# Attention and soft MoE on one core: half tiles after 12 products, three stores on GpSimd's queue, 48 TensorE instructions fewer

## The chip, the cores and the metric

The kernel runs on one core of a Trainium2 chip. The core has a matrix engine (TensorE, PE in the profile; its weight loads are PEld), a vector engine (VectorE, DVE), a scalar engine (ScalarE, ACT), GpSimd (POOL), and SyncE (SP), which here only issues DMAs. The engines run side by side and wait for each other by semaphores; 16 DMA engines move data between the chip's memory and the core. The metric is the device time of one launch in microseconds (us); the time given for a kernel is the median of its runs.

## The reference

Softcapped attention over 8 batches and 12 heads, then a soft mixture of experts over its result, cut to what is computed:

```python
scores = scale * np.matmul(q, k.transpose(0, 1, 3, 2))      # q, k, v: 8 x 12 x 448 x 64
scores = cap * np.tanh(scores / cap)
attn = np.exp(scores - max); attn = attn / (sum + 1e-09)
x = np.matmul(attn, v) ... reshape(3584, 768)
logits = x @ phi                                            # 32 slots: 8 experts, 4 slots each
slot_input = softmax_over_tokens(logits).T @ x
for e in range(8):                                          # w1: 768 x 1024, w2: 1024 x 768
    slot_out[e] = np.maximum(slot_input[e] @ w1[e], 0.0) @ w2[e]
out = softmax_over_slots(logits) @ slot_out                 # 3584 x 768, float32
```

## The kernel before

The order of the instructions on each engine is written out by hand: engines take them in the order in which the Python text emits them.

The attention part runs over 56 chunks of six score tiles. `run(j, slot)` emits what `at(j, slot, ...)` has put into a table for chunk `j` and a place in it. Some of that is unused work for PE: `spare(n, parts)` takes a PSUM tile of `parts` x 128 columns and lets `busy` (L880) write products of ones there that nobody reads. With `parts` of 1 each product has 128 columns; with 3, `n // 3` products have 384 and the rest 128. Each product is two PE instructions, a weight load and a matmul.

Behind the attention comes the mixture of experts, from L1054 on. The second weights are held in blocks of four: `w2_parts` lists half 0 (columns 0 to 383) and then half 1 (384 to 767) of 16 groups. The first 11 groups of half 0 lie in `w2b`; the other 5 and all 16 of half 1 are brought back from memory into `w2t` by 21 loads on SP's queue (L1059). `layer1` multiplies the slots with the first weights, `h_transp` turns the result, and `layer2(n0, half)` adds four products to the 128 x 384 accumulator `so_ps[half]`; a half takes 16 calls, 64 products. ACT copies the finished half 0 to `so[0]` (L1168), DVE half 1 to `so[1]` (L1177).

An output tile is 128 tokens by 768 columns, and there are 28. For the first `NH` = 12 of them the halves are made apart. The loop at L1170 runs half 1 of `layer2`, and six times, between its calls, it makes two half tiles of half 0, one finished by ACT and the next by DVE: a product with `so[0]` (L1148), a multiplication by the tokens' weights into a tile `obh` (L1150, L1152), a store of 192 KB on SP's queue (L1136). Before the change the first such pair stands behind 16 products of half 1 and the others 8 products apart. Behind the copy to `so[1]` the loop at L1182 makes half 1 of the same 12 tiles, stored two at a time, and then the 16 whole tiles (`ob`, L1193 to L1206). Each engine issues its own DMAs in order; SP has all stores.

Of the kernel before, what the change touches and what calls it, by code (L numbers as in the profile page):

```python
# [37 lines left out]
def kernel(  # L38
# [31 lines left out]
    pe, dve, act, pool, sp = nc.tensor, nc.vector, nc.scalar, nc.gpsimd, nc.sync  # L70
# [673 lines left out]
    def et_tile(bb, c):  # L744
        return (ETl if bb == B // 2 - 1 else ET4[:, bb])[:, c, :, :].rearrange("p a q -> p (a q)")
# [50 lines left out]
    def at(j, slot, f, *a):  # L796
        if j < 0:
            j, slot = 0, "b"
        aux.setdefault((j, slot), []).append((f, a))
# [24 lines left out]
    for b in range(B):  # L824
        j, p = b * PER, 6 * b
# [31 lines left out]
    for n, job in enumerate(wjobs):  # L857
        at(1 + n * (NCH - 5) // len(wjobs), "b", *job)
    for j, slot, n in ((0, "a", 5), (0, "c", 16), (1, "b", 12), (1, "c", 3)):
        at(j, slot, spare, n, 1)  # L860
    LATE = ((52, 'd', 3, 1), (54, 'd', 3, 3),)
    for j, slot, n, parts in LATE:
        at(j, slot, spare, n, parts)
    at(34, "<b", fill, 7)
# [86 lines left out]
    def bank(shape, dt=F32, name="bank"):  # L951
        n = turns.pop(0)
        if not turns:
            turns.extend((3, 2, 6, 0, 1))
        return big.tile(shape, dt, name=name, tag=f"b{n}")
# [149 lines left out]
    def layer2(n0, half):  # L1105
        for n in range(n0, n0 + 4):
            i, ft, gg = blocks[n]
            pe.matmul(so_ps[half][32 * gg:32 * gg + NS, :],  # L1108
                      hpad[:, 4 * i + gg, ft, :],
                      w2_half(n, half),  # L1110
                      start=(n0 == 0), stop=(n0 == len(blocks) - 4))
# [18 lines left out]
    so_ps += [bank([P, HD], name=f"so_ps{half}") for half in range(2)]  # L1130
    obs, waiting = {}, {}

    def store(n, h0, h1, src, tokens=1):
        bb, c = divmod(n, NT)
        width = (h1 - h0) * HD
        sp.dma_start(out=bass.AP(tensor=out.tensor,  # L1136
                                 offset=(2 * bb * S + c) * D + h0 * HD,
                                 ap=[[NT * D, P], [1, tokens * D]] if width == D else
                                 [[NT * D, P], [D, tokens], [1, width]]),
                     in_=src)  # L1140

    def half_tile(n, half, home, eng):

        bb, c = divmod(n, NT)
        if c == 0:
            obs[bb, half] = wts.tile([P, NT, HD], F32, name="obh", tag="w1", bufs=E)
        ob = obs[bb, half][:, c, :]
        pe.matmul(home, et_tile(bb, c), so[half], start=True, stop=True)  # L1148
        if eng == "dve":
            dve.tensor_scalar_mul(ob, home, winv[:, bb, c:c + 1])  # L1150
        else:
            act.mul(ob, home, winv[:, bb, c:c + 1])  # L1152
        k = waiting.pop(half, n)
        if half and n + 1 < NH and c < NT - 1 and k == n:
            waiting[half] = n
            return
        store(k, half, half + 1, obs[bb, half][:, c - (n - k):c + 1, :], n - k + 1)

    NH = 12
    n2 = len(blocks)  # L1160
# [8 lines left out]
    done = 0  # L1169
    for n0 in range(0, n2, 4):  # L1170
        layer2(n0, 1)

        if n0 % 8 == 4 and n0 > 4 and done < NH:
            for eng in ("act", "dve"):
                half_tile(done, 0, bank([P, HD], name="op0"), eng)
                done += 1
# [5 lines left out]
    for n in range(B // 2 * NT):  # L1182
        bb, c = divmod(n, NT)
        if n == NH + 3:
            e_transp(B - 1)
        if n == NH + 5:
            e_transp(B - 2)
        op = fin.tile([P, 2, 512], F32, name="op", tag="op")
        if n < NH:
            half_tile(n, 1, op[:, 0, 0:HD], "act" if n % 2 else "dve")  # L1190
            continue
        for half in range(2):
            pe.matmul(op[:, half, 0:HD], et_tile(bb, c), so[half],  # L1193
                      start=True, stop=True)

        if n == NH or c == 0 or full:
            ob, n1 = wts.tile([P, 2, 2, HD], F32, name="ob", tag="w1", bufs=E), n
        dst = ob[:, n - n1, :, :]
        if n % 2:
            dve.tensor_scalar_mul(dst, op[:, :, 0:HD], winv[:, bb, c:c + 1])  # L1200
        else:
            act.mul(dst, op[:, :, 0:HD], winv[:, bb, c:c + 1])  # L1202
        full = n > n1 or c == NT - 1
        if full:
            store(n1, 0, 2, ob[:, 0:n - n1 + 1, :, :].rearrange("p t a d -> p (t a d)"),
                  n - n1 + 1)  # L1206
# [35 lines left out]
```

## Time and profile before

| | us |
|---|---|
| median of 3 runs | 283.15 (282.86 to 283.71) |
| the profiled execution | 283.45 |
| span of its instructions | 281.7 |
| ACT busy | 249.1 (88%) |
| PE busy | 246.5 (88%) |
| DVE busy | 239.5 (85%) |
| POOL busy | 140.9 (50%) |
| attention part, up to about | 237 |
| mixture of experts up to the first half tile | 237 to 251 |
| output tiles and their stores | 251 to 280 |

The profile shows one execution. Each engine's rows give start, length, line and operation; "idle" is the time for which an engine had nothing to do just before, with the instruction that released it; "issue" stands where the profile shows no such instruction. In the windows the DMA share is the busy time of the 16 DMA engines over the stretch; packets overlap a little, so it can exceed 1. The queue called q1 is SP's and ACT's, q0 is GpSimd's, and q8 carries instructions.

### The profile page before, as it was taken

Reading aid. Unit: us, or ns where it says so; the run is one execution under the profiler, and the core shown is the slowest. Engines: PE = TensorE matmul, PEld = TensorE weight load, DVE = VectorE, ACT = ScalarE, POOL = GpSimd, SP = SyncE. Lnnn points to the kernel's source line nnn. Section 1 sums busy time; section 2 is a strip of 40 time slices with the busy share of each in tenths; the row PEclk is TensorE's granted clock in tenths of the full one; section 3 lists DMA queues with packets and bytes.
Section 4 is the critical chain, followed back from the end, with each engine's and each line's share of the span. In section 5 each row is a group of like instructions: output and inputs, shape, how many; then the busy total and the mean of one; then the engine's idle time right before and its main releaser. Section 6 shows DMA issues by size and latency. Waiting matters only on the chain.

```text
span 281.7 us, 10449 instructions
## 1 busy us (share of the span) xinstructions
PE 246.5 (88%) x4563; PEld 167.0 (59%) x4563; DVE 239.5 (85%) x474; ACT 249.1 (88%) x198; POOL 140.9 (50%) x198
## 2 busy tenths in 40 slices
PE   8897889998998999889998999899988999997720
PEld 7555556756665766566656675667565777642410
DVE  3479999999999999999999999999999996447840
ACT  3999999999999999999999999999999997236730
POOL 7885548662957285727673768285744120200000
PEclk9999999999999999999999999999999999999995
DMA  7999999999999999999999999999999589959997
GB/s 245 245 190 203 218 211 227 228 223 217 206 218 225 219 231 226 225 216 213 221 226 215 207 220 230 217 219 214 231 217 220 128 260 317 408 201 391 413 424 303
DMA packets 58332, 68.08 MB, mean 242 GB/s; under 512 B 4144, under 2 KB 54448, under 8 KB 58288
## 3 DMA queue, kind: packets, MB, share of 16 engines
q0 software_dynamic: 42448, 35.31, 79.7%
q1 hardware_dynamic: 15552, 31.89, 32.4%
q8 instruction: 35, 0.57, 0.7%
q10 hardware_dynamic: 288, 0.23, 0.3%
q14 instruction: 9, 0.07, 0.1%
HBM read 91.72 MB, written 19.27 MB: 394 GB/s over the span
## 4 chain that ended last, share of the span: by engine, by line
ACT 38%; PE 31%; DVE 20%; issue 5%; POOL 1%; DVEq 0%; ACTq 0%
ACT ex L374 16%; ACT ex L366 14%; PE pv L635 8%; ACT ex L362 7%; PE sc L349 4%; DVE xq L645 2%; DVE xp L615 2%; PE so_ps L1108 2%; PE hp L1080 2%; DVE xp L613 2%; DVE ex L616 2%; ACT ob L1202 2%; PE op L1193 1%; DVE xf L612 1%; PE op L1148 1%
## 5 line engine op out<-in xcount | busy, mean ns | idle before, releaser
L366 ACT ACTIVATE ex<-sc 128x1344 f16<-128x1344 f32 (+1 forms) x91 | 118.5, 1405 | 1.5 <-PE sc L349 1.5
L374 ACT ACTIVATE ex<-ex 128x1344 bf16<-128x1344 f16 (+5 forms) x58 | 110.2, 1911 | 0.1
L635 PE MATMUL pv<-vbd,ex 128*128 128x130 bf16 (+1 forms) x1610 | 95.0, 212 | 9.5 <-POOL vbd L289 3.9
L635 PEld LDWEIGHTS <-ex 128*128 128x128 bf16 (+1 forms) x1680 | 75.6, 101 | 38.1 <-issue 6.2
L289 POOL CAST vbd<-vraw 64x896 bf16<-64x896 f32 x46 | 47.3, 1027 | 60.2 <-PE pv L635 42.5
L349 PE MATMUL sc<-qT,kT 64*64 64x448 bf16 x672 | 66.4, 359 | 5.6 <-ACT ex L366 4.1
L349 PEld LDWEIGHTS <-kT 64*64 64x64 bf16 x672 | 22.4, 105 | 14.4 <-ACT ex L366 6.3
L645 DVE TENSOR_TENSOR xq<-pv,rec 128x448 bf16<-128x448 f32 x46 | 28.7, 625 | 1.6
L362 ACT ACTIVATE ex<-sc 128x2688 f16<-128x2688 f32 x11 | 28.1, 2552 | 0.1
L615 DVE TENSOR_TENSOR xp<-xp,xf 128x1344 f16<-128x1344 f16 (+2 forms) x34 | 27.5, 808 | 0.5
L616 DVE TENSOR_TENSOR ex<-ex,xp 128x1344 uint16<-128x1344 uint16 (+2 forms) x34 | 26.9, 791 | 0.2
L613 DVE TENSOR_TENSOR xp<-xf 128x1344 f16<-128x1344 uint16 (+2 forms) x34 | 26.9, 790 | 0.2
L116 POOL DMA_DIRECT2D w1b<-in_moe_w_dram x32 | 25.8, 808 | 0.0
L281 DVE COPY kT<-kps 128x896 bf16<-128x896 bf16 x23 | 14.2, 616 | 4.9 <-PE kps L276 2.8
L610 DVE TENSOR_SCALAR ex<-ex 128x1344 uint16<-128x1344 f16 (+2 forms) x34 | 17.0, 501 | 1.2 <-ACT ex L362 0.7
L614 DVE TENSOR_SCALAR xp<-xp 128x1344 f16<-128x1344 f16 (+2 forms) x34 | 17.0, 500 | 0.6
L612 DVE TENSOR_SCALAR xf<-ex 128x1344 uint16<-128x1344 uint16 (+2 forms) x34 | 17.2, 507 | 0.3
L185 POOL DMA_DIRECT2D qb<-in_q_dram x22 | 16.3, 739 | 1.5 <-PE qps L279 0.9
L297 POOL MEMSET vbd<- 64x1 bf16 x22 | 3.0, 138 | 27.7 <-PE pv L635 27.4
L617 DVE TENSOR_SCALAR ex<-ex 128x1344 uint16<-128x1344 uint16 (+2 forms) x34 | 16.5, 484 | 0.2
L185 POOL DMA_DIRECT2D kb<-in_k_dram x22 | 16.5, 748 | 0.0
L120 POOL DMA_DIRECT2D w2d<-in_moe_w_dram x21 | 16.1, 789 | 0.0
(124 smaller groups left out, 320.6 us busy)
## 6 DMA issues: line engine op xcount, KB each, us to landing
w1b<-in_moe_w_dram POOLq DMA_DIRECT2D x32, 384.0 KB, 9.6
vraw<-in_v_dram SPq DMA_DIRECT2D x44, 224.0 KB, 6.3
w2d<-in_moe_w_dram POOLq DMA_DIRECT2D x21, 384.0 KB, 9.7
w2t<-w2d SPq DMA_DIRECT2D x21, 384.0 KB, 6.5
out_dram<-ob SPq DMA_DIRECT2D x7, 768.0 KB, 6.8
qb<-in_q_dram POOLq DMA_DIRECT2D x22, 224.0 KB, 8.1
kb<-in_k_dram POOLq DMA_DIRECT2D x22, 224.0 KB, 7.7
w2b<-in_moe_w_dram POOLq DMA_DIRECT2D x11, 384.0 KB, 8.9
```

Of the source, the lines that this page charges most:

```text
L116: pool.dma_start(out=w1b[e][:, js, fs], in_=w1r[:, e, js, fs])
L185: pool.dma_start(out=t, in_=quad_ap(nm, Q))
L289: pool.tensor_copy(vbds[Q % 2][r, :, :, c0:c0 + DH], raw[r])
L349: ins = pe.matmul(sc[cs, u, 0:S], qkT["k", Q][r, c, cs], qkT["q", Q][r, :, cs], start=True, stop=True).ins
L362: apart["t", i - 1] = apart["t", i] = act.activation(exs[j].bitcast(F16), own["board"][:, :, 0:S], ACT.Tanh, scale=qk_scale / cap).ins
L366: ins = act.activation(exs[j][:, half * CS + u0:half * CS + u1, :].bitcast(F16), (own[0] if i == u0 == 0 else sc)[:, u0:u1, 0:S], ACT.Tanh ...
L374: act.activation(exs[j][:, u0:u1, :], exs[j][:, u0:u1, :].bitcast(F16), ACT.Exp, scale=cap)
L613: lambda: dve.tensor_tensor(p, s, s.bitcast(F16), op=ALU.mult),
L615: lambda: dve.tensor_tensor(p, p, s, op=ALU.mult),
L616: lambda: dve.tensor_tensor(y, y, p, op=ALU.add),
L635: pe.matmul(out_, exs[j][r, u, q0:q0 + (HP if tail else P)], v_, start=(c == 0 and g == gs[0] < NF), stop=(c == NT - 1), skip_group_check= ...
L645: dve.tensor_tensor(xq[Q][:, h, s0:s1, :], pv[:, 0:s1 - s0, 0:DH], rec.to_broadcast([P, s1 - s0, DH]), op=ALU.mult)
```

## The change

```diff
     for j, slot, n in ((0, "a", 5), (0, "c", 16), (1, "b", 12), (1, "c", 3)):
-        at(j, slot, spare, n, 1)
-    LATE = ((52, 'd', 3, 1), (54, 'd', 3, 3),)
+        at(j, slot, spare, n)
+    LATE = ((52, 'd', 3, 3), (54, 'd', 3, 3),)
...
-    def store(n, h0, h1, src, tokens=1):
+    def store(n, h0, h1, src, tokens=1, queue=None):
...
-        sp.dma_start(out=bass.AP(tensor=out.tensor,
+        (queue or sp).dma_start(out=bass.AP(tensor=out.tensor,
...
-        store(k, half, half + 1, obs[bb, half][:, c - (n - k):c + 1, :], n - k + 1)
+        store(k, half, half + 1, obs[bb, half][:, c - (n - k):c + 1, :], n - k + 1,
+              pool if n in (1, 3, 5) and not half else None)
...
-        if n0 % 8 == 4 and n0 > 4 and done < NH:
+        if n0 % 8 == 0 and n0 > 0 and done < NH:
```

Three things change. The unused products of chunks 0 and 1, and three of chunk 52, are emitted with 384 columns where three can be joined: 39 products become 15, which is 48 PE instructions fewer, all of them ahead of the mixture of experts. The six pairs of half tiles stand behind 12, 20, 28, 36, 44 and 52 products of half 1 instead of 16, 24, 32, 40, 48 and 56, so that the last pair has 12 products behind it instead of 8. And the half-0 stores of tiles 1, 3 and 5, the ones that DVE finishes in the first three pairs, are issued by GpSimd instead of SP.

## The prediction

> **What bounds the kernel now.** I read the page first, then the last 40 us in windows, the chain of waits and the timeline around the code that changes, and last the DMA queues in short windows. The page:
>
> ```profile
> span 281.7 us, 10449 instructions
> PE 246.5 (88%) x4563; PEld 167.0 (59%) x4563; DVE 239.5 (85%) x474; ACT 249.1 (88%) x198; POOL 140.9 (50%) x198
> ...
> DMA  7999999999999999999999999999999589959997
> ...
> q8 instruction: 35, 0.57, 0.7%
> ```
>
> ACT and DVE fill the attention part; the last slices belong to the DMA engines. The windows of that end (span, then busy time of PE, weight loads, DVE, ACT, POOL; granted clock, DMA share, GB/s) and the stores' rows:
>
> ```profile
> 246.00:249.50 3.50, 3.50 (x93) 2.15 (x81) 2.00 (x9) 0.47 (x1) 0.00 (x0) 1.00 0.91 358
> 249.50:252.50 3.00, 2.53 (x36) 0.80 (x35) 0.86 (x2) 1.47 (x3) 0.00 (x0) 1.00 0.11 38
> 253.00:254.00 1.00, 1.00 (x15) 0.35 (x18) 0.62 (x2) 0.71 (x2) 0.00 (x0) 1.00 0.82 306
> 254.00:258.00 4.00, 2.88 (x32) 0.86 (x27) 3.06 (x6) 2.15 (x4) 0.00 (x0) 1.00 1.05 393
> 258.00:265.00 7.00, 6.09 (x33) 2.93 (x33) 5.99 (x10) 5.43 (x9) 0.00 (x0) 1.00 1.07 401
> 266.00:280.00 14.00, 3.15 (x16) 1.35 (x15) 4.29 (x5) 3.49 (x4) 0.00 (x0) 0.82 1.00 415
> 280.00:281.70 1.70, 0.00 (x0) 0.00 (x0) 0.00 (x0) 0.00 (x0) 0.00 (x0) 0.50 0.00 2
> ...
> out_dram<-obh SPq DMA_DIRECT2D x14, 192.0 KB, 2.0
> ```
>
> From 254 to 280 the share is 1.0 or more and the rate 393 to 415 GB/s; then nothing moves until the program closes. So the end is set by the time of the first stored byte, plus the idle time of the DMA engines behind it, plus the transfer of 11.01 MB of output (3584 x 768 x 4 bytes): 24 half tiles of 0.197 MB at 401 GB/s make 11.8 us (0.49 us each), the other 6.29 MB at 415 GB/s 15.1 us, together 26.9 us. Ahead of it lies a hole of 3 us, 249.5 to 252.5, at 38 GB/s: weights have arrived, outputs have not begun. What ends the hole is the timeline (start, length, engine, line, operation) and, below the dots, the chain of waits:
>
> ```profile
> 248.48 1.14 PE L1108 MATMUL so_ps<-w2t,hpad 128*32 128x384 bf16 x21
> 249.52 0.48 ACT L1168 CAST so<-so_ps 128x384 bf16<-128x384 f32 x1 [2.53 <-PE so_ps L1108]
> 250.85 0.50 PE L1148 MATMUL op<-so,ET 128*128 128x384 bf16 x2
> 251.22 0.58 ACT L1152 ACTIVATE obh<-op,winv 128x384 f32<-128x384 f32 x1 [1.23 <-PE op L1148]
> 251.46 0.62 DVE L1150 TENSOR_SCALAR obh<-op,winv 128x384 f32<-128x384 f32 x1 [2.25 <-PE op L1148]
> 251.83 10.89 SPq L1136 DMA_DIRECT2D out_dram<-obh  x19
> ...
> 245.03 1.42 PE hp L1080 x48
> ...
> 247.40 2.22 PE so_ps L1108 x49
> 249.62 0.47 issue
> 250.09 0.83 PE so_ps L1108 x15
> 250.92 0.43 PE op L1148 x2
> 251.35 0.44 PE so_ps L1108 x8
> ...
> 256.27 0.56 DVE so L1177
> 256.83 0.05 issue
> 256.88 0.35 PE op L1148
> ```
>
> PE stands still at 249.62 and no engine is named. Five groups of half 0 come from w2t, which is 20 products, so the 21st in the first row is the first product of half 1; the 15 at 250.09 are its products 2 to 16. The stall thus cuts between two products of one group, where no new load, bank or vector result can be due. What remains is that PE had no next instruction. The page shows 35 instruction transfers with 0.57 MB, 16 KB each, for 9126 PE instructions: one per 261, so blocks of about 256 of 64 bytes. They can come late where PE is fast: the 49 products with their weight loads are 98 instructions in 2.2 us, so 256 take under 6 us.
>
> **The change part by part.** *Merged products.* Four calls in chunks 0 and 1 go from 36 products of 128 columns to 11 of 384 and 3 of 128 (22 less), one in chunk 52 from 3 to 1 (2 less): 24 products, with their weight loads 48 instructions. Columns stay the same:
>
> ```profile
> 10.22 1.07 PE L887 MATMUL junk<-ones 128*128 128x128 bf16 x16
> 15.87 0.82 PE L884 MATMUL junk<-ones 128*128 128x384 bf16 x4
> ...
> 6.44 2.54 ACT L366 ACTIVATE ex<-sc 128x448 f16<-128x448 f32 x3 [1.20 <-PE sc L349]
> ...
> ACT ex L366 <- PE sc L349: 1.5, 2, 1.2
> ```
>
> 16 narrow ones take 1.07 us; the 5 wide and 1 narrow that replace them, at about 0.2 each, 1.1: between -0.2 and +0.1 us of PE time. ACT covers it: in the whole kernel it waited 1.5 us for scores, 1.2 of them at 6.44, before its first tanh and ahead of all these products. Taken: 0. Without the cover it would be 0.2 us.
>
> What the 48 do change is where a block of instructions ends. If the 2nd product of half 1 was the first of a block, the block now begins 24 products later. In the new order half 1 runs 12 products, a pair of half tiles, 8 products, a pair (together 24): the boundary falls behind the first four half tiles. Its block is asked for later too, by 24 layer-1 products, about 0.7 us (48 take 1.42 us in the chain), so it arrives near 250.8; PE gets there at 251.4. I take no stall there; if it comes, it costs a part of 0.47 us, late in the ramp.
>
> *Half tiles four products earlier.* Half 1 begins near 249.3; 12 products at 2.22/49 us are done by 249.9. The half tile also needs `so[0]`, at 249.52 + 0.48 = 250.00, and 0.05 us to PE, as behind the other copy (256.83 to 256.88). So the first pair runs at 250.06, 0.79 us earlier than 250.85. Were the stall to stay ahead of it, only four products would be saved, half of 0.44: 0.22 us. Everything behind keeps its pace of 0.43 + 0.44 = 0.87 us per pair. Behind the last pair there are now 12 products instead of 8, and `so[1]` follows about 0.65 us earlier than at 256.27, so half 1 does not run dry.
>
> *Three stores on GpSimd's queue.* SP needs about 0.4 us for an issue, and a store's first byte follows at 252.65:
>
> ```profile
> L1136 SPq DMA_DIRECT2D out_dram<-obh x19: 337/408/846, 251.8 to 261.9; - x19
> ...
> GB/s 0 0 0 0 0 0 61 307 61 492 307 369 553 123 492 307 492 492 184 614 246 430 430 307 492 246 246 308 123 62 62 0 62 0 0 246 184 246 492 123
> ```
>
> (window 252.5 to 253.5, 25 ns a slice: 0.82 us from issue to first byte). What GpSimd needs for a store no row shows. Its nearest kin are its loads. First a timeline row; then the queues from 5 to 9.3 us, where q0, GpSimd's own, has no packet at all; then those from 5 to 10 us; last the medians of two equal loads, one from each queue:
>
> ```profile
> 5.48 0.82 POOL L185 DMA_DIRECT2D qb<-in_q_dram  x1 [0.22 <-DVE kT L238]
> ...
> q1 hardware_dynamic: 926, 1.57, 101.9%
> ...
> q0 software_dynamic: 87, 0.08, 9.7%
> ...
> kb<-in_k_dram POOLq DMA_DIRECT2D x22, 224.0 KB, 7.7
> vraw<-in_v_dram SPq DMA_DIRECT2D x44, 224.0 KB, 6.3
> ```
>
> So the bounds of issue to first byte are 1.3 us (SP's 0.82 and the 0.48 by which 0.82 exceeds 0.34) and 3.9 us (no packet between 5.48 and 9.3, but behind full engines). The medians differ by 1.4 us, which makes 0.82 + 1.4 = 2.2. The engines will be half idle, so I take 2.5, nearer to the medians.
>
> With it the DMA engines see: tile 0 from 251.86, tile 2 from 252.73, tile 4 from 253.60, each 0.49 us long and 0.87 apart, and tile 1, ready at 251.46 + 0.62 - 0.79 = 251.29, from 253.8 on. Idle: 0.38 + 0.38 = 0.76 us, then full. Before: 0.05 ahead of 253, 0.24 in the window to 254 (306 of 401 GB/s), and 0.1 since SP's issues paced eleven stores at 393 instead of 401 GB/s: 0.4 us. Change: -0.79 + 0.76 - 0.4 = -0.43 us. At 1.3 us tile 1 starts at 252.6, the idle time is 0.25 and the change -0.94; at 3.9 us tile 6 (254.47) comes first, idle 1.14 and the change -0.05. The transfer is what ends last in all three, so nothing is late behind them but the stores. On the queues: GpSimd is idle (0.00 in the windows), nothing waits behind its three issues, and SP's other stores move up.
>
> The Trainium skill ("DMA: Bandwidth & Descriptors", section "Latency and other measured facts") gives a first byte after about 1 us for GpSimd's path and 0.6 us for SP's. This trace has 0.82 for SP and over 3.8 for GpSimd's first load; by the page the three stores would cost nothing and the change would be near -1.1 us, 282.1.
>
> *The next block of instructions.* A read of 16 KB occupies one DMA engine:
>
> ```profile
> q8 instruction: 1, 0.02, 5.4%
> ...
> q8 instruction: 1, 0.02, 3.3%
> ```
>
> These are the windows 241.5 to 242.6 (0.054 x 16 x 1.1 = 0.95 us of one engine) and 250 to 252.6, where the kernel's last read falls into the hole. It will be asked for about 1.3 us later, 251.4 instead of 250.09, and so land among tiles 2 and 4, whose gaps take most of it. Priced at +0.1 us; bounds 0 and 0.95, if its engine has no gap.
>
> Sum: -0.43 + 0.1 = -0.33 us. The profiled execution took 283.45 us (span 281.7 and 1.75 around it), so 283.1; the median of the runs is 0.3 lower, 283.15, so **282.8 us**.
>
> **The rivals.** *GpSimd's stores start soon* (1.3 to 1.5 us): 283.15 - 0.94 = 282.2. For it: nothing else is in that queue. Against: the empty slot from 5.48 to 9.3.
>
> *The last read of instructions falls into full queues* and its engine carries 0.95 us to the end, since each store has its share on every engine: with slow GpSimd stores, 283.15 - 0.05 + 0.95 = 284.05, slower. It decides from a start of the read later than about 253.7, where idle time ends. For it: before, this read fell by luck into idle time. Against: it came 1 us after PE passed the boundary, which puts it at 252.4.
>
> *The stall does not move* since it is not one of instructions: the pair gains 0.22 instead of 0.79, and the loss on GpSimd's stores stays: -0.22 + 0.76 - 0.4 + 0.1 = +0.24, 283.4. Here the 48 instructions do nothing. The Trainium skill's "Runtime: NRT & Kernel Launch", section "Instruction fetch mechanics", speaks for it: blocks of 256 instructions, as the 35 transfers agree, are fetched ahead and a boundary is "mostly hidden". The stall at 249.62 with no releaser speaks against.
>
> **How the numbers follow.** A measurement of this kernel can tell about 0.3% (0.85 us) from no change, so faster is below 282.3 and slower above 284.0. Forecast 0.44 (its own range 282.3 to 283.2), early GpSimd stores 0.30, late read 0.16, stall unmoved 0.10. Faster: the 0.30 and 0.05 of the forecast's edge, 0.35; slower: the 0.16 and 0.02 of the last, 0.18; same 0.47. The range reaches from early stores with their full -0.94 and the spread of the runs (281.9) to the late read (284.1).
>
> **What would show it.** Right: PE runs 12 products of half 1 without a stall and the first half tile starts near 250.1; the DMA windows show load from 252 with gaps until about 253.8; the last stores land about 0.3 us earlier relative to their first byte plus 27 us. Wrong: an issue gap still ahead of the first half tile; the first GpSimd bytes within 1.5 us or after 3.5; one engine's landings about 1 us behind the others' up to the end; or ACT waiting for scores in chunks 0 to 2.

## The result, and the profile after

The changed kernel takes 283.55 us in the median of 22 runs (282.44 to 285.05), the kernel before 282.73 us in 22 runs on the same chip (282.02 to 283.71). The ratio is 1.0029 [1.0017, 1.0041]: 0.8 us slower, where 0.3 us faster was forecast. The two profiled executions are closer, 283.45 before and 283.62 after, each with a span of 281.7 us. The one before, from which the prediction was worked out, is 0.7 us above its kernel's median; the one after is at its own.

The page of the changed kernel: span, busy times, DMA share in 40 slices, and the queue that carries instructions.

```profile
span 281.7 us, 10401 instructions
PE 245.7 (87%) x4539; PEld 165.9 (59%) x4539; DVE 240.4 (85%) x474; ACT 249.1 (88%) x198; POOL 142.0 (50%) x201
...
DMA  7999999999999999999999999999999489959996
...
q8 instruction: 35, 0.57, 0.8%
```

PE has 24 products less, ACT is as busy as before and DVE 0.9 us busier, and there are still 35 reads of instructions. The chain of waits (start, length, what) in the ramp:

```profile
247.22 2.09 PE so_ps L1108 x48
249.32 0.02 issue
249.34 0.49 ACT so L1169
249.83 0.04 issue
249.87 0.48 PE op L1148 x2
```

The stall at 249.62 is gone. What the first half tile waits for now is ACT's copy to `so[0]`, and it starts at 249.87 where 250.06 was forecast. The first two rows below are windows that the prediction showed of before; then come four of the end, and the same four of the kernel before (columns as there; DMA share and GB/s stand last).

```profile
249.50:252.50 3.00, 2.91 (x39) 0.82 (x32) 1.60 (x3) 2.01 (x4) 0.89 (x2) 1.00 0.21 70
254.00:258.00 4.00, 2.77 (x28) 0.94 (x21) 3.27 (x6) 2.07 (x5) 0.00 (x0) 1.00 1.00 375
...
278.00:279.00 1.00, 0.00 (x0) 0.00 (x0) 0.00 (x0) 0.00 (x0) 0.00 (x0) 0.50 0.94 378
279.00:279.50 0.50, 0.00 (x0) 0.00 (x0) 0.00 (x0) 0.00 (x0) 0.00 (x0) 0.50 0.23 86
279.50:280.00 0.50, 0.00 (x0) 0.00 (x0) 0.00 (x0) 0.00 (x0) 0.00 (x0) 0.50 0.06 25
280.00:280.50 0.50, 0.00 (x0) 0.00 (x0) 0.00 (x0) 0.00 (x0) 0.00 (x0) 0.50 0.02 6
```

```profile
278.00:279.00 1.00, 0.00 (x0) 0.00 (x0) 0.00 (x0) 0.00 (x0) 0.00 (x0) 0.50 0.96 396
279.00:279.50 0.50, 0.00 (x0) 0.00 (x0) 0.00 (x0) 0.00 (x0) 0.00 (x0) 0.50 1.03 418
279.50:280.00 0.50, 0.00 (x0) 0.00 (x0) 0.00 (x0) 0.00 (x0) 0.00 (x0) 0.50 0.47 184
280.00:280.50 0.50, 0.00 (x0) 0.00 (x0) 0.00 (x0) 0.00 (x0) 0.00 (x0) 0.50 0.02 6
```

Before, all DMA engines work until about 279.75. After, the share falls to 0.23 at 279 and to 0.06, one of 16, until 280. A store's landing is recorded in 16 parts, and each is taken here for one DMA engine. After, 14 engines have landed their part of the last store by 279.6, the last two at 280.03 and 280.52; before, 15 had by 280.20 and the last at 280.62. So most of the output was done half a microsecond earlier, and the end is where it was. The late engine's lag begins at the start. This is the stretch from 251.3 to 252.5 of the changed kernel in 40 slices (30 ns each), with its queues:

```profile
DMA  0000009000005397999989896969561100000000
GB/s 0 0 0 0 0 0 546 0 0 0 0 0 205 154 358 307 410 358 410 358 307 461 307 461 256 512 256 512 205 206 52 52 0 0 0 0 0 0 0 0
...
q1 hardware_dynamic: 135, 0.18, 41.1%
q8 instruction: 1, 0.02, 8.8%
```

The read of 16 KB begins at 251.50 (the lone 546: its bytes are booked in the slice where it begins) and takes 0.088 x 16 x 1.2 = 1.69 us, to 253.19; the first store's bytes shown here run from 251.68 to 252.25. By the landing records 15 engines have put down their part of this store by 252.69, the 16th only at 254.52.

### The profile page after: what moved, and what is told of

Its sections match the earlier page's. It is cut to its first block, busy times and chain, and to the rows that moved or that the text cites. A ratio compares the mean times of both kernels' runs of the same rounds, so it can differ in the third digit from the quotient of the medians.

```text
span 281.7 us, 10401 instructions
## 1 busy us (share of the span) xinstructions
PE 245.7 (87%) x4539; PEld 165.9 (59%) x4539; DVE 240.4 (85%) x474; ACT 249.1 (88%) x198; POOL 142.0 (50%) x201
## 4 chain that ended last, share of the span: by engine, by line
ACT 35%; DVE 28%; PE 26%; issue 5%; DMA 1%; POOL 1%; DVEq 0%; SPq 0%; ACTq 0%
ACT ex L374 14%; ACT ex L366 12%; ACT ex L362 7%; PE pv L635 6%; PE sc L349 4%; DVE xq L645 4%; DVE xp L615 3%; DVE xp L613 3%; DVE xf L612 2%; DVE ex L616 2%; DVE ex L610 2%; DVE qT L281 2%; PE hp L1080 2%; DVE ex L617 2%; PE so_ps L1108 2%
## 5 line engine op out<-in xcount | busy, mean ns | idle before, releaser
L366 ACT ACTIVATE ex<-sc 128x1344 f16<-128x1344 f32 (+1 forms) x91 | 116.9, 1374 | 1.5 <-PE sc L349 1.5
L374 ACT ACTIVATE ex<-ex 128x1344 bf16<-128x1344 f16 (+5 forms) x58 | 108.6, 1878 | 0.1
L616 DVE TENSOR_TENSOR ex<-ex,xp 128x1344 uint16<-128x1344 uint16 (+2 forms) x34 | 26.9, 791 | 0.2
L614 DVE TENSOR_SCALAR xp<-xp 128x1344 f16<-128x1344 f16 (+2 forms) x34 | 17.7, 520 | 0.6
```

What stands on the lines that cost most here:

```text
L366: ins = act.activation(exs[j][:, half * CS + u0:half * CS + u1, :].bitcast(F16), (own[0] if i == u0 == 0 else sc)[:, u0:u1, 0:S], ACT.Tanh ...
L374: act.activation(exs[j][:, u0:u1, :], exs[j][:, u0:u1, :].bitcast(F16), ACT.Exp, scale=cap)
L616: lambda: dve.tensor_tensor(y, y, p, op=ALU.add),
```

## Theories

- **R**: the last read of instructions now falls among the first stores. Each store has its share on every DMA engine (its landing comes in 16 parts), so the engine that reads is late, and either SP is held up in its next issue, with all engines idle, or that engine ends last.
- **G**: GpSimd's stores make an engine late.
- **P**: the merged products disturb the attention part itself.
- **S**, on the gain: the stall of the profiled execution before isn't in every execution, so there was less to win than 0.79 us.

## The experiments

Ratios, with 95% intervals in brackets, are to the kernel before, measured together with the others of the same group; its medians in the four groups were 282.77 (35 runs), 282.69 (29), 282.65 (30) and 282.88 us (30). A ratio is not the quotient of the two medians shown. The parts of the change are called merging, early half tiles and GpSimd's stores.

**The three parts alone.** Merging alone:

```diff
-        at(j, slot, spare, n, 1)
-    LATE = ((52, 'd', 3, 1), (54, 'd', 3, 3),)
+        at(j, slot, spare, n)
+    LATE = ((52, 'd', 3, 3), (54, 'd', 3, 3),)
```

> The kernel before with the 48 TensorE instructions fewer alone; half tiles and stores as before. Theory R (the last 16 KB read of TensorE's instructions moves from the hole ahead of the stores into the stores, and the one DMA engine that serves it ends about 1 us late): first half tile near 250.1, most engines done 0.7 us earlier than before, one engine alone for about 1 us at the end, time 283.0 to 283.6 against 282.7. Theory G (the stores on GpSimd's queue are what makes one engine late): the stall is gone and nothing is lost, 282.0. Theory P (the wide products disturb the attention part): 283.5 with the loss ahead of 237 us.

Early half tiles alone:

```diff
-        if n0 % 8 == 4 and n0 > 4 and done < NH:
+        if n0 % 8 == 0 and n0 > 0 and done < NH:
```

> The kernel before with the half tiles four products earlier alone. All theories: the stall stays ahead of the first pair, which comes 0.2 us earlier; the last read of instructions stays in the hole; 282.5 against 282.7, no lone engine of more than 0.5 us at the end.

GpSimd's stores alone:

```diff
-        store(k, half, half + 1, obs[bb, half][:, c - (n - k):c + 1, :], n - k + 1)
+        store(k, half, half + 1, obs[bb, half][:, c - (n - k):c + 1, :], n - k + 1,
+              pool if n in (1, 3, 5) and not half else None)
```

> The kernel before with the three stores on GpSimd's queue alone. Theory R: the last read stays in the hole, so at most the gaps of the first stores cost something, 282.7 to 283.1. Theory G: one engine 1 us late to the end, 283.5.

Measured: merging 283.52 us, 1.0014 [0.9991, 1.0038]; early half tiles 282.91, 0.9991 [0.9972, 1.0010]; GpSimd's stores 283.11, 1.0004 [0.9984, 1.0024]. Only merging has a median well above the one before, though its interval doesn't settle it. Its profile does show how: the row of SP's issues (min/mean/max in ns), then the DMA engines in the window 250 to 255 in slices of 125 ns.

```profile
L1136 SPq DMA_DIRECT2D out_dram<-obh x18: 338/408/2128, 250.4 to 261.5; - x18
```

```profile
DMA  1111111000699999993000000000000018999999
```

One issue, at 251.48, took 2.13 us instead of 0.4. The read of instructions ran from 251.50 to 253.23, that issue ended at 253.61, and from 252.4 to 254 the other engines stood idle after two stores. R had the time (283.0 to 283.6) but not the form: it expected one engine alone for about 1 us at the end, and the last store's parts land close together, 14 by 280.41 and all by 280.69. Early half tiles bring nothing that shows, where 282.5 was expected. With GpSimd's stores alone SP's first three issues take 0.33 to 0.34 us and no engine is late (the 15th lands at 279.30, the last at 279.60), which speaks against G.

**Two parts.** Merging and early half tiles, which is the change without GpSimd's stores:

> The changed kernel with all stores on SP. Theory R: as the changed kernel, one engine alone for about 1 us at the end, 283.2 to 283.6. Theory G: the first stores 0.8 us earlier and no late engine, 282.0.

Early half tiles and GpSimd's stores, which is the change without merging:

> The changed kernel with the 48 TensorE instructions put back: half tiles earlier and three stores on GpSimd's queue. Theory R (the read of 16 KB of instructions that comes about 1 us after TensorE passes a block boundary occupies one DMA engine for 1 to 1.7 us; SP cannot issue more than two stores past it, and that engine's share of every store stays late): the stall ahead of the first pair is back unless the read before it comes early, and the last read ends by about 252.5, so SP's longest early issue is under 0.8 us; 282.3 to 282.9, against the changed kernel's 283.55. Theory G (GpSimd's stores): 283.4 as the changed kernel.

The first took 283.28 us, 1.0001 [0.9983, 1.0019], with one SP issue of 1.49 us in its profile; the second 282.96, 1.0014 [0.9998, 1.0030], just above the 282.3 to 282.9 that R allowed, with none above 0.41 us among SP's first six stores. By medians the first loses to the second, by ratios not: neither interval decides, and the first run's ratio doesn't show the cost that its profile has (table below).

**More instructions, not fewer.** All unused products that are otherwise joined are emitted with 128 columns, early half tiles and GpSimd's stores kept: 100 PE instructions more than before. The edit is against the changed kernel.

```diff
-            at(j + 1, "d", spare, 14)
-            at(j + 2, "d", spare, 5)
+            at(j + 1, "d", spare, 14, 1)
+            at(j + 2, "d", spare, 5, 1)
...
-                at(j + k, slot, f, n)
+                at(j + k, slot, f, n, *((1,) if f is spare else ()))
...
-        at(j, slot, spare, n)
-    LATE = ((52, 'd', 3, 3), (54, 'd', 3, 3),)
+        at(j, slot, spare, n, 1)
+    LATE = ((52, 'd', 3, 1), (54, 'd', 3, 1),)
...
-    spare(6)
+    spare(6, 1)
...
-    busy(3)
+    busy(3, junk[:, 0:P])
...
-    busy(6)
+    busy(6, junk[:, 0:P])
```

> Half tiles and GpSimd's stores as changed, and unused products emitted singly, 100 TensorE instructions more than before. A block boundary then falls at the 15th product of half 0, where the block has more time to arrive, and the next one 128 products later, near the end of half 1. Theory R: no stall ahead of the first pair, a read near 250 in the hole, SP's third issue under 0.6 us; 36 instruction reads in place of 35, the added one near 256 to 258 among the stores, with one engine about 1 us late at the end; 282.3 to 282.9. Theory G: one engine 1 us late from the first stores on, 283.5.

284.77 us, 1.0073 [1.0051, 1.0095], far above the 282.3 to 282.9 that R gave: R had the added read and the late engine, and put no time on them. The profile has one read more, which falls into the full transfer, from 255.95 to 257.18. The page's queue, and two windows:

```profile
q8 instruction: 36, 0.59, 0.8%
```

```profile
254.00:256.00 2.00, 1.82 (x24) 0.46 (x22) 1.49 (x4) 1.16 (x2) 0.10 (x1) 1.00 0.93 351
256.00:258.00 2.00, 1.13 (x5) 0.50 (x6) 1.57 (x3) 0.69 (x2) 0.00 (x0) 1.00 0.91 333
```

During that read one SP issue, at 256.26, takes 1.31 us, and 333 GB/s are moved where the changed kernel moves 397. From the first stored byte (252.18) to the last landing (281.53) it takes 29.35 us, 1.1 more than the same stores without such a read (28.2, table below), and at the end one engine lands 0.9 us behind the others.

**Fewer of the 48, by steps.** Early half tiles with 12 or 24 instructions less:

```diff
-    for j, slot, n in ((0, "a", 5), (0, "c", 16), (1, "b", 12), (1, "c", 3)):
-        at(j, slot, spare, n, 1)
-    LATE = ((52, 'd', 3, 1), (54, 'd', 3, 3),)
+    for j, slot, n, parts in ((0, "a", 5, 3), (0, "c", 16, 1), (1, "b", 12, 1), (1, "c", 3, 3)):
+        at(j, slot, spare, n, parts)
+    LATE = ((52, 'd', 3, 3), (54, 'd', 3, 3),)
```

> Half tiles earlier, all stores on SP, and only 12 TensorE instructions fewer (calls of 5 and 3 products in chunks 0 and 1 and the one of chunk 52). The boundary falls 6 products behind its old place, so TensorE reaches it at about 249.7. Theory R: a stall of 0.3 to 0.7 us there at most, the read 0.3 us earlier than before or the same, ending by 252.3; first half tile 250.1 to 250.6; 282.3 to 282.8. If only the count mattered and not the read's place, as changed without GpSimd's stores, 282.9 to 283.3.

```diff
-    for j, slot, n in ((0, "a", 5), (0, "c", 16), (1, "b", 12), (1, "c", 3)):
-        at(j, slot, spare, n, 1)
+    for j, slot, n, parts in ((0, "a", 5, 3), (0, "c", 16, 3), (1, "b", 12, 1), (1, "c", 3, 1)):
+        at(j, slot, spare, n, parts)
```

> As the last, with 24 instructions fewer (calls of 5 and 16 products in chunk 0). The boundary falls behind the 12 products, at the first pair of half tiles. Theory R: first half tile near 249.9, a short stall at most, the read 250.6 to 251.6; SP's third issue blocked for less than 1 us; 282.2 to 282.8.

12 less: 282.58 us, 0.9990 [0.9979, 1.0002]; the read ends at 251.39, ahead of the first stored byte at 251.50. 24 less: 283.03, 1.0015 [0.9999, 1.0032]; it ends at 251.76, 0.57 us behind the first byte, and one SP issue takes 1.25 us. R had allowed 282.2 to 282.8 and less than 1 us of waiting, so it undercounted a read that overlaps the stores only in part.

**The same 12 without early half tiles, and with GpSimd's stores.**

> 12 TensorE instructions less (6 unused products) and nothing else: the block boundary lies 6 products later than before, half tiles stay where they were (from the 16th product of half 1 on). Theory R: the read ends 0.6 us or more before the first stored byte plus 0.8, no SP issue over 0.8 us, no engine late; 282.3 to 282.8 us, ratio 0.998 to 1.000. Rival P (the merged products themselves disturb the attention part): a cost in proportion, a quarter of what all 48 cost, 282.8 to 283.1 us. Rival: the last read falls later than in the kernel with earlier half tiles, because PE reaches the boundary at the same time while nothing else moved: then an SP issue over 1 us and 283.0 to 283.5 us.

> Earlier half tiles, three stores on GpSimd's queue, 12 TensorE instructions less: the change with a quarter of its merged products. Theory R: the read ends before or with the first stored byte (250.2 to 251.4 us in the kernel without GpSimd), so no engine is late; what is left is the gaps that GpSimd's stores leave, 0.2 to 0.4 us: 282.7 to 283.0 us, ratio 1.000 to 1.001. Theory G (GpSimd's stores make one engine late): as the whole change, 283.4 to 283.6 us, one engine 0.6 us or more behind the others at the end.

12 less alone: 282.71 us, 1.0003 [0.9987, 1.0019], the read over at 250.52. The rival of a later read isn't there. No cost in proportion shows, though the interval is too wide to exclude P by itself; nor is there a gain. With early half tiles and GpSimd's stores: 282.96, 1.0000 [0.9984, 1.0017]. G expected 283.4 to 283.6. The late engine that it expected isn't there: the 15th lands at 280.20, the last at 280.56. This run shows something else, the block boundary. First the kernel with early half tiles alone, then this one, in the chain of waits:

```profile
247.43 2.22 PE so_ps L1108 x49
249.65 0.77 issue
250.42 0.67 PE so_ps L1108 x11
```

```profile
247.23 2.39 PE so_ps L1108 x55
249.62 0.48 issue
250.10 0.50 PE so_ps L1108 x5
```

With 12 instructions, or 6 products, taken away far ahead, PE stops 6 products later. So the stall hangs on the place in PE's stream of instructions and not on what the product needs, as a missing block of instructions would; no row names the block. Counted in PE's own order the last read hangs on the same place: in 17 of the 18 profiles, all but that of the 100 more, the last read ahead of the stores' end starts 0.3 to 1.3 us after PE begins its 4437th product, whichever product that is. It is the one at which PE went on at 250.09 in the first profile of before.

**Both kernels again.**

> The kernel before, unchanged, for a second profile. What it tells: whether the 0.47 us stall ahead of half 1's first half tile, from whose removal the forecast took 0.79 us, belongs to every run of it. Theory S (the stall depends on when the read of 16 KB of instructions before it lands, which differs from one execution to the next): it may be anything from 0 to 0.9 us, the first half tile starts 9.4 to 10.3 us after the first layer-1 product, and the execution takes 282.0 to 283.5 us, the less the smaller the stall. Rival (the stall is fixed by where the block ends in the program): 0.4 to 0.6 us again, first half tile 10.1 to 10.3 us after the first layer-1 product, 283.2 to 283.7 us.

> The kernel after, unchanged, for a second profile. Theory R (the last read of instructions falls among the first stores and holds one of the 16 DMA engines): no stall ahead of the first half tile (9.3 to 9.6 us after the first layer-1 product); the read starts 0.3 us before to 0.5 us after the first stored byte and lasts 0.9 to 1.8 us; either one of SP's issues takes over 1 us or one engine's last landing lies 0.6 us or more behind the others'; 283.2 to 283.9 us. Rival G (GpSimd's stores): the late engine is there also where the read ends before the first stored byte.

Before: 282.74 us (8 runs), profiled execution 283.11, span 281.0. Its chain:

```profile
247.45 3.01 PE so_ps L1108 x64
250.46 0.43 PE op L1148 x2
```

No issue row; the 64 products take 3.01 us where the kernel with 12 less alone has 2.71, so 0.30 us of stall is left of 0.81 (2.22 + 0.47 + 0.83 = 3.52 in the first profile). The chain of 12 less alone:

```profile
246.96 2.71 PE so_ps L1108 x64
249.68 0.43 PE op L1148 x2
```

That is theory S in kind: the same program, a different stall. The time fits less well, since 283.11 is again above the median. After: 284.30 (3 runs), 1.0057 [1.0032, 1.0081], above the 283.9 that R allowed. In the profiled one the first layer-1 product came at 241.70, 1.2 us later than in the first profile; that part of it lies in the attention, ahead of all that is studied here. The read came late as well, from 253.39 to 254.49, 0.51 us behind the first byte, and two engines land at 281.11 and 281.16 where 14 are done by 280.66. That is 0.5 us where R asked for 0.6, and SP's issue during this read took 0.33 us, so R's two signs show only weakly here.

**The count put back, or taken away, elsewhere.** Up to here the count was only lowered in chunks 0, 1 and 52, so P had a way out. In the first kernel the change stays whole, and 48 instructions come back in six batches of unused products between chunks 13 and 48:

```diff
-                at(j + k, slot, f, n)
+                at(j + k, slot, f, n, *((1,) if f is spare and 0 < b < 7 else ()))
```

> The kernel after, with 48 TensorE instructions put back at another place: the unused products of chunks 0 and 1 stay merged, and seven-column-block unused products of chunks 13 to 48 are issued singly in six batches. Theory R (only the count ahead of half 1 matters, since it puts the block boundary): as the kernel with earlier half tiles, GpSimd's stores and the 48 in their old place, 282.7 to 283.2 us, ratio 1.000 to 1.002; the last read of instructions ends before or with the first stored byte. Rival P (the merging in chunks 0 and 1 costs by itself): as the kernel after, 283.4 to 283.7 us, ratio 1.0025 or more.

In the second the kernel before stays, and 40 instructions go from the warm-up at the very start and from chunk 52:

```diff
-    busy(27)
+    busy(27, boots[1][:, 0, 0:3 * P])
...
-    LATE = ((52, 'd', 3, 1), (54, 'd', 3, 3),)
+    LATE = ((52, 'd', 3, 3), (54, 'd', 3, 3),)
```

> The kernel before, with 40 TensorE instructions less at other places than the change's: the 27 narrow warm-up products at the very start become 9 wide ones of the same columns (36 less), and one unused product of chunk 52 is merged as in the change (4 less). Theory R: the last read of instructions starts 1.3 to 2.0 us after the first half tile product, so among or after the first stores; an issue of SP over 1 us or one engine late, first stored byte to last landing 28.4 to 29.4 us instead of 27.8 to 28.0; 283.1 to 283.6 us, ratio 1.001 to 1.003. Rival P: no cost, 282.7 us, ratio 1.000.

Beside them the changed kernel itself, and the one with early half tiles and 12 less once more:

> The kernel after, on the same chip and in the same rounds as the kernel with 48 instructions put back elsewhere. Theory R: 283.4 to 283.9 us, ratio 1.002 to 1.004, and above that kernel by 0.4 us or more. Rival: no difference from it, which would leave GpSimd's stores as the cost.

> Earlier half tiles and 12 instructions less, again: is it faster than the kernel before by more than a measurement can tell? Theory R: its read ends before or with the first stored byte, so it keeps at most what the stall costs in the runs that have one: ratio 0.998 to 1.000. Rival (it is the version that beats both): below 0.998.

The changed kernel took 283.93 us, 1.0043 [1.0027, 1.0059]; with 48 put back elsewhere it took 282.90, 1.0014 [0.9998, 1.0029]. Chunks 0 and 1 are the same in both: 0.0029, or 0.8 us (1.0 us by the medians), goes with the count. The kernel before with 40 taken away in the warm-up took 283.62, 1.0031 [1.0015, 1.0047]; nothing that the change touches has a part in it but the joined products of chunk 52. P falls, R holds, with two times just above what it gave (to 283.6 and 283.9). The profiles agree: the first layer-1 product starts at 240.4 us in the mean of the seven with 24 or more instructions less, and at 240.6 in the others, so nothing is lost in the attention. The last kernel took 282.44, 0.9986 [0.9973, 1.0000], the best of all; both of its intervals end at or beyond 1, so it is not clear of the kernel before.

The window 250 to 255 in slices of 125 ns, and the row of SP's issues: first of the kernel with 40 less in the warm-up, then of the one with 48 put back.

```profile
DMA  0000000000006028999999700000000799999999
```

```profile
L1136 SPq DMA_DIRECT2D out_dram<-obh x19: 338/414/1469, 251.0 to 261.9; - x19
```

```profile
DMA  3931100001000000029997009694989937794989
```

```profile
L1136 SPq DMA_DIRECT2D out_dram<-obh x16: 332/411/833, 251.4 to 261.7; - x16
```

In the first the read lies at 251.62 to 253.02, and after two stores all engines are idle for 1 us, to 253.9; SP's long issue ended at 253.39. In the second the read (250.24 to 251.67) is over before the first byte at 252.19; the small gaps are there in every kernel with GpSimd's stores, and the 0.83 us issue comes after 255, when the queues are full anyway.

## Why the prediction was wrong

All profiled executions side by side, us, worked out from the trace's packet records: how far the end of the last read lies behind the first stored byte, and the time from that byte to the last landing. G marks GpSimd's stores.

```
                              read's end       first byte to
                              - first byte     last landing
12 less alone                    -0.91            27.76
before, second profile           -0.42            27.76
early half tiles                 -0.39            27.82
early, 12 less, second           -0.52            27.84
before                           -0.17            27.95
early, 12 less                   -0.11            28.00
early, 24 less                   +0.57            28.54
40 less in the warm-up           +1.19            28.68
early and merging                +1.39            28.70
merging                          +1.97            29.42
G alone                          -0.39            28.17
G, early, 12 less                +0.02            28.21
G, all, 48 put back              -0.52            28.22
G, early                         -0.32            28.23
G, all: after, second            +1.61            28.28
G, all: after, third             +1.18            28.56
G, all: after                    +1.51            28.84
```

- **What bounds the end: right.** From the first stored byte on it is transfer plus idle time: 26.9 us of transfer, and where nothing disturbs it 27.8 to 28.0, with the gaps and up to 0.48 us from the last byte to its landing.
- **Merged products at no PE time: right.** With 48 put back elsewhere they cost nothing that shows. The step that they move a block boundary by 24 products was right too: PE passes its 4437th product 2.6 us ahead of the first stored byte in the two profiles of before, and 0.52 us ahead in all three of the changed kernel, where 251.4 against 251.86 was forecast.
- **"-0.79": right in the trace, wrong as a gain.** Against the profiled execution the first half tile came earlier by 0.80 us, measured from the first layer-1 product (10.17 to 9.37). But all of it is the stall. In the kernel with 12 less alone the half tiles still stand behind 16 products, and there is no stall: its half tile also comes 9.37 us after that product. The 16 products end (2.71 us after the first) just when ACT's copy lets 12 go (2.09 + 0.02 + 0.49 + 0.04 = 2.64). So placing half tiles four products earlier is worth under 0.1 us, and the change can win only what the stall costs: 0.81 in one profile of before, 0.30 in the other, and these executions lie 0.7 and 0.4 us above the medians. The prediction took one execution's stall for the kernel's. It even had the time of the copy, 250.00, but asked only what the pair would wait for after the change, not what it would have waited for before without the stall.
- **Three stores on GpSimd's queue: price right by luck.** Taken was a first byte 2.5 us after the issue, within 1.3 to 3.9, and 0.76 us of gaps instead of 0.4. The first byte came 1.14 us after the issue, below both bounds:

```profile
251.38 0.56 POOL L1136 DMA_DIRECT2D out_dram<-obh  x1 [9.26 <-DVE obh L1150]
```

```profile
q0 software_dynamic: 10, 0.05, 109.6%
```

The first is the timeline's row of the issue, the second GpSimd's queue in the window 252.5 to 252.6; from 251.3 to 252.5 it had no packet. Bounds from two loads that met full engines were no bounds for an idle queue. The Trainium skill ("DMA: Bandwidth & Descriptors", section "Latency and other measured facts") has about 1 us, and this trace agrees. What did not follow was its sum, 282.1: with the read out of the way the kernels with GpSimd's stores have 28.17 to 28.23 us from first byte to last landing, the others 27.76 to 28.00. The gaps cost 0.35 us (means 28.21 and 27.86), and 0.36 was forecast. By the packet records the first MB is stored 3.25 us after the first byte there and after 2.6 to 2.9 us in the others, so the gaps lie near the start; the 0.25 us of idle time that the prediction gave for a first byte after 1.3 us was too little. So the rival of early stores was right on the latency and wrong on the time (its 282.2 also left out the 0.1 for the read).
- **"Priced at +0.1 us": this step failed most.** The place of the read was right: it was to land among tiles 2 and 4, behind the first stored byte, and it ended 1.2 to 1.6 us behind that byte, having started at 251.50, 251.40 and once at 253.39, 0.2 us ahead of the byte to 0.5 behind it. The price was not. Its upper bound, 0.95, came from another read; the prediction's second row gives 0.033 x 16 x 2.6 = 1.37 us for the very read that was to move. "Whose gaps take most of it" holds for an engine that can catch up, and the prediction let trouble start only from 253.7, where idle time ends. In fact the read holds its engine for 0.88 to 1.73 us, and a store isn't done until that engine has done its part. With SP's stores alone the other engines run dry: 28.54 to 29.42 us, 0.7 to 1.6 more than where the read is out of the way (27.86). An issue of SP that stands during the read ends shortly behind it: 0.37 to 0.45 us in merging, 40 less and the changed kernel, 0.16 to 0.53 over all profiles that have one. With GpSimd's stores the others go on and one or two engines end last: 28.28 to 28.84 against 28.2. The Trainium skill ("Runtime: NRT & Kernel Launch", section "Instruction fetch mechanics") calls the crossing of a block "mostly hidden"; in this stretch the traces don't agree, since PE stood 0.2 to 0.9 us at a block's end in five of them. The rival "late read" thus came closest in its mechanism, 284.05 with 0.16, but on its own condition it would not have applied. By number the unmoved stall, 283.4, was nearer to 283.55; that is luck, as the stall had gone. Two of the prediction's signs of being wrong did appear: GpSimd's first byte within 1.5 us, and one engine about 1 us behind at the end (0.95 and 0.85 us in two of the three profiles).

Put together for the changed kernel: 0.35 us for GpSimd's gaps and, by the runs, 0.8 for the read, against a stall that in the median run is worth some tenths; measured were 0.8 us more in 22 runs, 1.05 in 8 and 1.65 in 3. Two things stay open. The stall's mean size isn't to be had from two profiles. And the three profiles of the changed kernel show only 0.1 to 0.6 us of the read's 0.8; the third, with 0.35, was the fastest of its eight runs (282.81), so the profiles may not be typical, but that wasn't shown.

A kernel whose last read stays out of the output's way whatever the count wasn't tried, and why SP's issue waits for one engine stays open too.

## What to carry to other kernels

Where a tail is bound by transfers, a change in the number of PE's instructions anywhere ahead of it moves where the next block of instructions is read; look for that read in the short windows, and count a read that falls among the first stores with up to its full length (here 0.7 to 1.6 us for reads of 1.05 to 1.73 us), since every store needs the engine that it holds. A stall seen in one profile is worth what the median run has of it: take a second profile before counting it as a gain, and ask what would release the work if the stall alone were gone.

## What the runs showed of the hardware

- PE came out of a long stall 2.3 to 2.4 us after the last read ahead of it had started (reads at 247.65, 248.11 and 247.76; PE going on at 250.09, 250.42 and 250.10), though these reads lasted only 0.9 us. That this read brought the missing block is inferred from the steady distance. Whether there is a stall ahead of the first half tile, in the kernels that have a block boundary there, goes with when that read started after the first layer-1 product: 6.97 to 7.40 us in the three executions with 0.65 us or more, 6.58 and 6.60 in those with 0.21 and 0.30, 6.49 and less where there was none.
- Among the first stores SP's issue can take 1.07 to 2.13 us instead of 0.34 to 0.4 while one DMA engine is held by a read of instructions (five profiles, 0.82 in a sixth); in the second profile of the changed kernel it did not. Later, with the queues full, issues of up to 1.2 us occur in every kernel.
- GpSimd's store has its first byte 1.14 us after the issue, the same in all eight profiled executions that have such stores, SP's 0.84 to 0.85.
